# One planner change in a causal-attention-plus-gated-MLP kernel: the softmax sums' small constant added by a reduction, eight filler matmuls after the first scores, new TensorE costs and 66-column loads

## Chip, cores and metric

One NeuronCore of a Trainium2 chip runs the whole program. The metric is the device time of one execution in microseconds (us), lower is better; the time before is a median of three runs.

## What is computed

Causal attention over 4 batches, 12 heads, 448 positions and head size 64; the 12 heads' outputs, side by side, are the 768 inputs of a gated MLP with 1536 hidden units.

```python
scores = scale * np.matmul(q, k.transpose(0, 1, 3, 2))
scores = np.where(mask, -1000000000.0, scores)
scores = scores - np.max(scores, axis=-1, keepdims=True)
attn = np.exp(scores)
attn = attn / (np.sum(attn, axis=-1, keepdims=True) + 1e-09)
x = np.matmul(attn, v)            # heads side by side: (1792, 768)
g = x @ w_gate
out = (g * (1.0 / (1.0 + np.exp(-g))) * (x @ w_val)) @ w_out
```

All tensors are float32. The products are made either in plain f32 or from a high and a low part in the faster fp32r type ("split" products of three matmuls each).

## The kernel before

The work is cut into four chunks, one per batch (CHUNKS, line 23). A chunk first needs the attention of its 12 heads, and then the MLP on 448 columns. A "unit" is one head of one batch (48 units), and two neighbouring heads form a pair.

**Attention of a unit.** The 448 query rows are cut at 0, 64, 192, 320, 448. TensorE writes the scores of a pair into PSUM tiles S (lines 502 and 505; the two heads sit in different halves of the rows of the array, so their matmuls run side by side). In batch 0 the scores are plain f32 (tiles qraw and kraw); in batches 1 to 3 they are split products (QS and KS). The DVE adds the mask and takes the row maximum (lines 527 and 553, with a read-out of m), ACT takes the exponential and leaves each row's sum in one column of a shared tile (line 565, `sums`), and then `recip` (lines 573 to 577) makes the reciprocals. The normalisation p times rec runs on ACT, POOL or DVE (lines 592, 596, 609, 613). TensorE transposes p into PSUM tiles T (lines 667 and 699), these are copied out as ph (ACT or DVE, lines 311 and 314) with a low part pl (DVE, line 333), and the product with V goes to PSUM tile O (line 741, or 772 in batch 0).

`recip` is two DVE instructions on a 128x4 (or 128x3) piece:

```python
sm, rc = sums[u % NR][:, i0:i1], rec[u % NR][:, i0:i1]
nc.vector.tensor_scalar(rc, sm, 1.0e-9, None, ALU.add)
nc.vector.reciprocal(rc, rc)
```

**MLP of a chunk.** 24 blocks of gate and value weights and 12 of output weights, each of six k-steps; a k-step is three matmuls 128x448 (lines 874 to 876, PSUM tiles M and MO). In chunk 0 each weight block is loaded (wide, line 848), unpacked (top and wraw, lines 311 or 317 and 857), split into whl, and stored to DRAM; later chunks load the split form again (line 826).

**What sets the order.** A planner (class Planner, line 83) gets all operations with the engines on which each may run, a cost on each, a due time and dependencies, and places them greedily; the instructions are then issued in the planned order with no further reordering, each engine in its own fixed order. `cost` (line 62) prices an operation, TURN (line 42) adds a price on TensorE for going from one kind of work to another, CAPS gives the number of buffers. The T tiles of batches 1 to 3 share one PSUM bank: the next transposes wait until ph and pl of the last ones have been made.

**Start.** WARM = 22 small bf16 matmuls on a tile of ones (line 280) run on TensorE until the first q and k have been loaded; then come the scores of the first pair and those of the second. The first pair's scores are issued in three sessions (FIRST, line 53).

**Short loads.** Where only 64 columns of stationary operand are needed, FEW = 72 columns are loaded (lines 504 and 739): in the scores of the first query block of batches 1 to 3, and in the three products of each unit with pl.

Of the kernel before, what the change touches and what calls it, by code (L numbers as in the profile page):

```python
# [8 lines left out]
F32 = mybir.dt.float32  # L9
# [4 lines left out]
BF16 = mybir.dt.bfloat16  # L14
AF = mybir.ActivationFunctionType
ALU = mybir.AluOpType

P = 128
D = 64
# [1 line left out]
CUTS = [[0, 64, 192, 320, 448], [0, 64, 192, 320, 448], [0, 64, 192, 320, 448], [0, 64, 192, 320, 448]]  # L21
WID = [0, 64, 192, 320, 448]
CHUNKS = [[(0, 0, 448)], [(1, 0, 448)], [(2, 0, 448)], [(3, 0, 448)]]
NR = 8
SLOPE0 = 1.0
WLEAD = 1.2
XD = [-10.0, 3.0]
# [11 lines left out]
SHARED = 0.5  # L39
PVLATE = 0  # L40
LAT = {"PE": 0.29, "DVE": 0.2, "ACT": 0.23, "POOL": 0.2, "SP": 0.1}
TURN = {'ms': 0.19, 'sm': 0.19, 'mt': 0.0, 'tm': 0.0, 'ts': 0.19, 'st': 0.19, 'mv': 0.15, 'vm': 0.15, 'tv': 0.15, 'vt': 0.15, 'sv': 0.15, 'vs': 0.15, 'om': 0.055, 'os': 0.1, 'so': 0.19, 'ot': 0.03}
TS = 0.0
PF = 1.12
GF = 1.25
# [2 lines left out]
TV = 0.0  # L48
WINDOW = 96
SPARE = [2]  # L50
FEW = 72
WARM = 22
FIRST = [[[0, 1]], [[2]], [[3]]]
KBUS = 1 / 320
DLAT = 1.8
# [8 lines left out]
def cost(e, kind, n):  # L64
    if e == "ACT":
        return {"psum": 66, "sbuf": 110, "ptr": 190, "exp": 280, "tanh": 160}[kind] / 1e3 + n / 1200
    if e == "DVE":
        return 0.075 + n / {"one": 1920}.get(kind, 960)
    if e == "POOL":
        return {"one": 190, "ptr": 260, "two": 180}[kind] / 1e3 + n / {"two": 465.0}.get(kind, 1200.0)  # L70
    return {"r": max(n * 0.4475e-3 + 0.0025, 0.109), "n": n / 600, "t": n * 0.109 / 128}[kind] + 0.001


class Res:
# [154 lines left out]
def kernel(  # L229
# [8 lines left out]
    nc = tc.nc  # L238
# [3 lines left out]
    NW, _, WC = wP.shape  # L242
    NF = 12
    NKC = len(CUTS[0]) - 1
# [18 lines left out]
    masks = cpool.tile([P, P + maskX + P], F32, tag="masks", name="masks")  # L263
    back, mask = masks[:, : maskX + P], masks[:, P:]
    both = cpool.tile([P, D], F32, tag="both", name="both")
    all_sums = cpool.tile([P, NR, NKC], F32, tag="sums", name="sums")
    sums = [all_sums[:, i] for i in range(NR)]
    all_rec = cpool.tile([P, NR, NKC], F32, tag="rec", name="rec")
    rec = [all_rec[:, i] for i in range(NR)]
    xs = [cpool.tile([P, T], F32, tag=f"xs{i}", name=f"xs{i}") for i in range(KD)]  # L270
    xh = [cpool.tile([P, T], F32R, tag=f"xh{i}", name=f"xh{i}") for i in range(KD)]
# [4 lines left out]
    ones = xs[0][:, : P // 2]  # L276
    nc.vector.memset(ones, 1.0)
    warm = bank("O", "warm")
    for _ in range(WARM):
        nc.tensor.matmul(warm[:, :P], ones.bitcast(BF16), ones.bitcast(BF16), start=True, stop=True)  # L280
    cpool.tile([P, 32], F32, tag="pad", name="pad")
    top = cpool.tile([P, WC], U32, tag="top", name="top")
    nc.vector.memset(top, 0)
    nc.vector.memset(all_sums, 1.0)
    make_identity(nc, ident)
    nc.gpsimd.memset(masks, 0.0)
    for m_, step, base in ((back, 1, 1 - P), (mask, -1, maskX)):
# [10 lines left out]
    def op(alts, due, deps=(), alloc=(), uses=(), extra=0.0):  # L298
        first = [heads[r.tag] for r in alloc if r.tag in heads]
        o = pl_.op(alts, due, list(deps) + first, alloc, uses, extra)  # L300
        o.soft = first
        o.port = bool(alts.pop("port", False))
        o.kb = alts.pop("kb", 0)
        o.kind = alts.pop("kind", "m")
        for r in alloc:
            heads[r.tag] = o
        return o
# [84 lines left out]
    def attention(u):  # L392
# [76 lines left out]
        if h % 2 == 0:  # L469
            if not U.ns:  # L470
                rQ, rK = Res("QS"), Res("KS")
                sp = []
                for nm, r_, src, ld, rr in (("Q", rQ, "q", lq, rq), ("K", rK, "k", lk, rk)):
                    def newsp(nm=nm):
                        s[nm] = buf([P, 2, S], F32R, nm + "S", nm + "S", f"{nm}S{u}")
                        return s[nm][:, 0]
                    x1 = op(copies("sbuf", N, newsp, lambda src=src: s[src + "w"]), due(0), [ld], [r_], [rr])
                    sp.append(op(binary(N, lambda nm=nm: s[nm][:, 1], lambda src=src: s[src + "w"],
                                        lambda nm=nm: raw(s[nm])[:, 0]), due(1), [x1], [], [r_, rr]))
            for gi_, sess in enumerate(FIRST if rest else SG if c == 0 else [sum(SG, [])]):  # L480
                tags = ["S", "X"] if c else ["SXM"[gi_]] if rest else ["MS"[gi_ == 0]]
                rSs = {(y, x): Res(tags[x]) for x in range(len(sess)) for y in (0, 1)}
                steps = sorted(sum(sess, []))

                def score(gi_=gi_, sess=sess, steps=steps, tags=tags):
                    passes = ((None, None),) if U.ns else ((0, 0), (0, 1), (1, 0))
                    for x, blks in enumerate(sess):
                        for y in (0, 1):
                            B_, off = bank(tags[x], f"S{u + y}_{gi_}_{x}"), 0
                            for i in blks:  # L490
                                q1_ = U.qi[i][1][1]
                                st[u + y][f"S{i}"] = B_[:, off : off + q1_]
                                off += q1_
                    for i in steps:
                        q0, q1_ = U.qi[i][1]
                        for z, (a, b_) in enumerate(passes):
                            for y in (0, 1):
                                half = slice(D * y, D * y + D)
                                Q = s["qw"][half] if U.ns else s["Q"][half, a]
                                K = s["kw"][half] if U.ns else s["K"][half, b_]  # L500
                                if U.joint and i == 0:
                                    nc.tensor.matmul(st[u]["S0"][half], Q[:, :D], K[:, :D] if y else K[:, S - D :], start=True, stop=True)
                                    continue
                                r = max(U.rows[i], FEW)
                                nc.tensor.matmul(st[u + y][f"S{i}"][:r], Q[:, q0 : q0 + r],  # L505
                                                 K[:, :q1_] if y else K[:, S - q1_ :], start=z == 0, stop=z == len(passes) - 1)
                ws = [U.qi[i][1][1] for i in steps]
                if U.ns:
                    so = op({"PE": (sum(cost("PE", "n", w) + 0.06 for w in ws) + TS, score), "kind": "s"}, due(2),
                            (rest if gi_ else some) or [lq, lk], list(rSs.values()), [rq, rk])  # L510
                else:
                    so = op({"PE": (sum(3 * cost("PE", "r", w) for w in ws) + TS, score), "kind": "s"}, due(2), sp,
                            list(rSs.values()), [rQ, rK])
                for x, blks in enumerate(sess):
                    for i in blks:
                        for y in (0, 1):
                            scored[u + y, i] = (so, rSs[y, x])
# [54 lines left out]

        def recip():
            i0, i1 = U.own[0][0], U.own[-1][0] + 1
            sm, rc = sums[u % NR][:, i0:i1], rec[u % NR][:, i0:i1]
            nc.vector.tensor_scalar(rc, sm, 1.0e-9, None, ALU.add)
            nc.vector.reciprocal(rc, rc)  # L577
        rc = op({"DVE": (0.3, recip)}, due(5), exps, [], [rsum])

# [138 lines left out]
    def weigh(u):  # L718
# [6 lines left out]
        if not npv:  # L725
            rO, dps, use, dur = Res("O"), [], [], 0.0
            for g, o_, w, _, stk, d_, r_ in (blocks[j] for j in range(nj)):
                dps += [x for x in d_ if x not in dps]
                use += [r for r in r_ if r not in use]
                dur += (1 if stk else 2) * cost("PE", "r", w)  # L730

            todo = [(j, "ph") for j in (0, *range(2, nj))] + [(j, "pl") for j in range(nj - 1, 0, -1)] + [(1, "ph")]

            def pv():
                s["O"] = bank("O", f"O{u}")


                for x, (j, t) in enumerate(todo):
                    g, o_, w, _, stk, _, _ = blocks[j]
                    m = FEW if t == "pl" else 2 * D  # L740
                    nc.tensor.matmul(s["O"][:m, U.base(j) - U.qa : N], s["VS"][:, j, :m], s[f"{t}{g}"][:, o_ : o_ + w],  # L741
                                     start=x == 0, stop=x == len(todo) - 1)
            last = op({"PE": (dur, pv), "kind": "o"}, due(10), dps, [rO], use)
            rx, rt = Res(f"xs{h}"), Res("tmp")

            def newt():
                s["tmp"] = buf([D, S], F32, "tmp", "tmp", f"tmp{u}")[:, :N]
                return s["tmp"]
            t1 = op(copies("psum", N, newt, lambda: s["O"][D:P, :N], engines="AD"), due(11), [last], [rt], [rO])
            o = op(binary(N, lambda: xs[k][D * (h % 2) : D * (h % 2) + D, :N], lambda: s["O"][0:D, :N],  # L750
                          lambda: s["tmp"], ALU.add, engines="D"), due(12), [t1] + prevx, [rx], [rO, rt])
            xs_ops.setdefault((c, k), []).append(o)
            xs_res.setdefault((c, k), []).append(rx)
            return
# [261 lines left out]
```

## Time and profile before

| | us |
|---|---|
| median of 3 runs (lowest, highest) | 683.66 (683.42, 683.88) |
| the profiled execution | 684.65 |
| its span, first to last instruction | 682.9 |
| PE (TensorE matmul) busy | 671.8 |
| DVE busy | 356.7 |
| ACT busy | 347.8 |
| POOL (GpSimd) busy | 193.7 |

The profile is of one execution; its time is 0.99 us above the median and 1.75 us longer than its span. Matmuls are pipelined, so PE's busy share is not its distance from the peak: the spacing of the starts of two matmuls is what a matmul costs. A row of the timeline shows start, duration, engine, line, operation, tiles, shape, count, and in brackets how long the engine had been idle and who released it.

### The profile page before, as it was taken

How to read it: one execution, taken by the hardware profiler on the slowest of the kernel's cores; microseconds unless marked ns; L12 is line 12 of the kernel's file. 1: busy time of each engine (PE TensorE's matmuls, PEld its weight loads, DVE VectorE, ACT ScalarE, POOL GpSimd, SP SyncE). 2: the span in 40 equal slices, each digit the busy share in tenths (PEclk: the TensorE clock that was granted, in tenths of full speed). 3: DMA queues.
4: the chain of work that ended last, by engine and by line, in shares of the span. 5: the costliest groups of instructions: out<-in, count | busy, mean ns of one | idle time of the engine just before them, and what ended most of it. 6: DMA issues, size and time to landing. Idle time of an engine off the chain costs nothing.

```text
span 682.9 us, 10861 instructions
## 1 busy us (share of the span) xinstructions
PE 671.8 (98%) x3898; PEld 598.9 (88%) x3898; DVE 356.7 (52%) x881; ACT 347.8 (51%) x864; POOL 193.7 (28%) x238
## 2 busy tenths in 40 slices
PE   9999999999999999999999999999999999999998
PEld 6567898899888999999999989999999999999997
DVE  5777889898788464355633346545444222222100
ACT  6998688687798363245634336346345211111000
POOL 3766455556162130031322214134232000000000
PEclk9999999999999999999999999999999999999999
DMA  8878899999988865556667665554555675676771
GB/s 293 277 260 308 303 352 390 321 374 314 347 309 324 320 202 201 191 176 215 202 223 239 201 230 189 200 186 139 186 198 164 216 224 213 223 229 212 226 251 41
DMA packets 40118, 165.08 MB, mean 242 GB/s; under 512 B 4480, under 2 KB 13952, under 8 KB 40064
## 3 DMA queue, kind: packets, MB, share of 16 engines
q1 hardware_dynamic: 39904, 164.28, 70.6%
q8 instruction: 31, 0.51, 0.3%
q14 instruction: 23, 0.19, 0.1%
q10 hardware_dynamic: 160, 0.10, 0.1%
HBM read 130.55 MB, written 33.82 MB: 241 GB/s over the span
## 4 chain that ended last, share of the span: by engine, by line
PE 81%; ACT 11%; DVE 6%; issue 1%; POOL 0%; ACTq 0%; DVEq 0%
PE M L874 15%; PE M L875 15%; PE M L876 15%; PE MO L874 8%; PE MO L875 8%; PE MO L876 7%; PE S L505 4%; PE O L741 4%; ACT p L565 4%; PE T L699 3%; ACT p L609 2%; ACT ph L311 1%; ACT top L311 1%; DVE wraw L857 1%; PE T L667 1%
## 5 line engine op out<-in xcount | busy, mean ns | idle before, releaser
L874 PE MATMUL M<-xh,whl 128*128 128x448 f32 x576 | 215.0, 373 | 0.0
L875 PE MATMUL M<-xl,whl 128*128 128x448 f32 x576 | 209.4, 364 | 0.0
L876 PE MATMUL M<-xh,whl 128*128 128x448 f32 x576 | 209.1, 363 | 0.0
L874 PEld LDWEIGHTS M<-xh,whl 128*128 128x128 f32 x576 | 108.2, 188 | 8.5 <-issue 1.7
L876 PEld LDWEIGHTS M<-xh,whl 128*128 128x128 f32 x576 | 108.1, 188 | 7.7
L875 PEld LDWEIGHTS M<-xl,whl 128*128 128x128 f32 x576 | 108.4, 188 | 6.8 <-DVE xl L333 0.3
L874 PE MATMUL MO<-hh,whl 128*128 128x448 f32 x288 | 107.2, 372 | 0.0
L876 PE MATMUL MO<-hh,whl 128*128 128x448 f32 x288 | 104.6, 363 | 0.6 <-DVE whl L333 0.6
L875 PE MATMUL MO<-hl,whl 128*128 128x448 f32 x288 | 104.7, 364 | 0.0
L565 ACT ACTIVATE p<-p,m 128x192 f32<-128x192 f32 (+3 forms) x180 | 91.1, 509 | 3.4 <-DVE m L553 3.3
L311 ACT ACTIVATE ph<-T 128x384 fp32r<-128x384 f32 (+3 forms) x116 | 57.8, 504 | 56.5 <-PE T L667 34.4
L553 DVE CUSTOM_DVE_ANT_0 p<-S,masks 128x192 f32<-128x192 f32 (+3 forms) x180 | 68.3, 426 | 21.4 <-PE S L505 20.2
L311 ACT ACTIVATE hh<-t 128x448 fp32r<-128x448 f32 x40 | 23.1, 577 | 82.0 <-DVE t L917 82.0
L609 ACT ACTIVATE p<-p,rec 128x192 f32<-128x192 f32 (+3 forms) x130 | 58.8, 502 | 9.3 <-DVE rec L577 9.0
L911 DVE SCALAR_TENSOR_TENSOR t<-t,M 128x448 f32<-128x448 f32 x48 | 29.7, 619 | 57.2 <-ACT t L907 56.8
L876 PEld LDWEIGHTS MO<-hh,whl 128*128 128x128 f32 x288 | 54.0, 188 | 4.7 <-DVE whl L333 1.0
L874 PEld LDWEIGHTS MO<-hh,whl 128*128 128x128 f32 x288 | 54.1, 188 | 4.5 <-issue 1.2
L875 PEld LDWEIGHTS MO<-hl,whl 128*128 128x128 f32 x288 | 54.2, 188 | 3.6 <-DVE hl L333 0.3
L917 DVE TENSOR_TENSOR t<-t,M 128x448 f32<-128x448 f32 x48 | 29.6, 618 | 51.0 <-PE M L876 50.6
L907 ACT ACTIVATE t<-M 128x448 f32<-128x448 f32 x48 | 26.0, 542 | 57.5 <-PE M L876 56.9
L333 DVE TENSOR_TENSOR pl<-T,ph 128x384 fp32r<-128x384 f32 x72 | 39.6, 550 | 22.6 <-ACT ph L311 22.3
L699 PE MATMUL T<-ident,p 128*128 128x128 f32 x288 | 46.8, 276 | 3.3 <-DVE pl L333 3.0
(80 smaller groups left out, 822.7 us busy)
## 6 DMA issues: line engine op xcount, KB each, us to landing
whl<-ws SPq DMA_DIRECT2D x108, 768.0 KB, 4.4
wide<-in_w_dram SPq DMA_DIRECT2D x36, 768.0 KB, 6.8
ws<-whl SPq DMA_DIRECT2D x36, 768.0 KB, 7.5
vraw<-in_v_dram SPq DMA_DIRECT2D x24, 256.0 KB, 4.3
out_dram<-osb SPq DMA_DIRECT2D x24, 224.0 KB, 4.7
qraw<-in_q_dram SPq DMA_DIRECT2D x23, 224.0 KB, 4.6
kraw<-in_k_dram SPq DMA_DIRECT2D x23, 224.0 KB, 4.6
qraw<-in_q_dram SPq DMA_DIRECT2D x1, 128.0 KB, 2.5
```

The source lines that it names most:

```text
L311: nc.scalar.activation(out(), in_(), AF.Copy, scale=scale)
L333: r["DVE"] = (cost("DVE", "two", n), lambda: nc.vector.tensor_tensor(out(), a(), b(), alu))
L505: nc.tensor.matmul(st[u + y][f"S{i}"][:r], Q[:, q0 : q0 + r], K[:, :q1_] if y else K[:, S - q1_ :], start=z == 0, stop=z == len(passes) - 1)
L553: nc.vector.tensor_tensor_reduce(p[:r], s[f"S{i}"][:r], mask[:r, maskX - q0 : maskX - q0 + q1_] if h % 2 else back[:r, P - min(q1_, P) : P ...
L565: nc.scalar.activation(p[:r], p[:r], AF.Exp, bias=peak(i)[:r], scale=-1.0, accum_out=sums[u % NR][:r, i : i + 1],)
L609: nc.scalar.activation(p[:r], p[:r], AF.Copy, scale=rec[u % NR][:r, i : i + 1])
L699: nc.tensor.transpose(pt[:, o_ + q0 - bs : o_ + q0 - bs + r], s[f"p{i}"][:r, k0 : k0 + P], ident[:r, :r])
L874: nc.tensor.matmul(out[:, :n], a[:, w], xhi, start=first, stop=False)
L875: nc.tensor.matmul(out[:, :n], a[:, w], xlo, start=False, stop=False)
L876: nc.tensor.matmul(out[:, :n], l[:, w], xhi, start=False, stop=last)
L911: nc.vector.scalar_tensor_tensor(t, t, 1.0, ps[c, f, 0][:, :N], ALU.add, ALU.mult)
L917: nc.vector.tensor_tensor(t, t, ps[c, f, 1][:, :N], ALU.mult)
```

## The change

`recip` no longer adds 1e-9 with a tensor_scalar. The tile of sums gets one more slot that holds 1e-9 in every element, the ring of slots for units goes from 8 to 7 so that the tile keeps its size, and a tensor_reduce adds slot u % 7 and the last slot. Eight more of the small matmuls on ones are issued behind the scores of the first pair. FEW goes from 72 to 66. And the planner gets other numbers for TensorE: the TURN table, a price of 0.062 for score matmuls of 64 columns, and a price without a floor ("f") for the products with V.

```diff
-NR = 8
+NR = 7
-TURN = {'ms': 0.19, 'sm': 0.19, 'mt': 0.0, 'tm': 0.0, 'ts': 0.19, 'st': 0.19, 'mv': 0.15, 'vm': 0.15, 'tv': 0.15, 'vt': 0.15, 'sv': 0.15, 'vs': 0.15, 'om': 0.055, 'os': 0.1, 'so': 0.19, 'ot': 0.03}
+TURN = {'ms': 0.15, 'sm': 0.17, 'mt': 0.0, 'tm': 0.0, 'ts': 0.15, 'st': 0.17, 'mv': 0.15, 'vm': 0.15, 'tv': 0.15, 'vt': 0.15, 'sv': 0.15, 'vs': 0.15, 'om': 0.0, 'os': 0.1, 'so': 0.16, 'ot': 0.0}
-FEW = 72
+FEW = 66
 WARM = 22
+WARM2 = 8
-    return {"r": max(n * 0.4475e-3 + 0.0025, 0.109), "n": n / 600, "t": n * 0.109 / 128}[kind] + 0.001
+    return {"r": max(n * 0.4475e-3 + 0.0025, 0.109), "f": n * 0.4475e-3 + 0.0045, "n": n / 600, "t": n * 0.109 / 128}[kind] + 0.001
...
-    all_sums = cpool.tile([P, NR, NKC], F32, tag="sums", name="sums")
+    all_sums = cpool.tile([P, NR + 1, NKC], F32, tag="sums", name="sums")
...
-    for _ in range(WARM):
-        nc.tensor.matmul(warm[:, :P], ones.bitcast(BF16), ones.bitcast(BF16), start=True, stop=True)
+
+    def busy(n):
+        for _ in range(n):
+            nc.tensor.matmul(warm[:, :P], ones.bitcast(BF16), ones.bitcast(BF16), start=True, stop=True)
+
+    busy(WARM)
...
-    nc.vector.memset(all_sums, 1.0)
+    nc.vector.memset(all_sums[:, :NR], 1.0)
+    nc.vector.memset(all_sums[:, NR], 1.0e-9)
...
+                    if u == 0 and i in FIRST[-1][0]:
+
+                        busy(WARM2)
...
-                    so = op({"PE": (sum(3 * cost("PE", "r", w) for w in ws) + TS, score), "kind": "s"}, due(2), sp,
+                    so = op({"PE": (sum(3 * (0.062 if w == D else cost("PE", "r", w)) for w in ws) + TS, score), "kind": "s"}, due(2), sp,
...
-            sm, rc = sums[u % NR][:, i0:i1], rec[u % NR][:, i0:i1]
-            nc.vector.tensor_scalar(rc, sm, 1.0e-9, None, ALU.add)
+
+            sm, rc = all_sums[:, u % NR :: NR - u % NR, i0:i1], rec[u % NR][:, i0:i1]
+            nc.vector.tensor_reduce(rc, sm.rearrange("p a c -> p c a"), mybir.AxisListType.X, ALU.add)
             nc.vector.reciprocal(rc, rc)
...
-                dur += (1 if stk else 2) * cost("PE", "r", w)
+                dur += (1 if stk else 2) * cost("PE", "f", w)
```

The planner's new numbers move instructions on every engine. Three places follow, as the built programs have them; line numbers of the changed kernel are 3 to 10 higher than the same line before.

First, TensorE at the start, from the last scores of the first pair (S_2) to the first of the second pair (S_0). Before:

```order
L505 MATMUL S_1_0_262<-kraw_230,qraw_228 128x320
L505 MATMUL S_2_0_272<-kraw_230,qraw_228 128x448
L505 MATMUL S_2_0_273<-kraw_230,qraw_228 128x448
L502 MATMUL S_0_0_291<-kraw_240,qraw_238 64x64 x2
L505 MATMUL S_0_0_291<-kraw_240,qraw_238 128x448
```

and in the change, of which the first of eight load-and-matmul pairs on ones is shown:

```order
L511 MATMUL S_1_0_263<-kraw_231,qraw_229 128x320
L511 MATMUL S_2_0_273<-kraw_231,qraw_229 128x448
L511 MATMUL S_2_0_274<-kraw_231,qraw_229 128x448
L283 LDWEIGHTS xs_71
L283 MATMUL warm<-xs_71 128x128
```

Eight such pairs now stand between the two pairs' scores; the second pair's scores follow them in the same order as before.

Second, the DVE at units 36 and 37 (batch 3): the copy ph36_1 of the first transposes, then the reciprocals of unit 37, then the low part pl36_1, for which the next transposes T36_2 wait. Before:

```order
L314 TENSOR_SCALAR ph36_1_4682<-T36_1_4673 128x384
L576 TENSOR_SCALAR rec_70<-sums_69 128x4
L577 RECIPROCAL rec_70<-rec_70 128x4
L333 TENSOR_TENSOR pl36_1_4690<-T36_1_4673,ph36_1_4682 128x384
L314 TENSOR_SCALAR ph36_2_4706<-T36_2_4697 128x384
```

and in the change:

```order
L320 TENSOR_SCALAR ph36_1_4691<-T36_1_4682 128x384
L586 TENSOR_REDUCE rec_70<-sums_69 128x4
L587 RECIPROCAL rec_70<-rec_70 128x4
L339 TENSOR_TENSOR pl36_1_4699<-T36_1_4682,ph36_1_4691 128x384
L320 TENSOR_SCALAR ph36_2_4715<-T36_2_4706 128x384
```

The places in the row are the same; only the kind of the first instruction of `recip` differs.

Third, the DVE at unit 12 (batch 1, the first unit with split products). Before:

```order
L314 TENSOR_SCALAR ph12_1_1051<-T12_1_1043 128x384
L576 TENSOR_SCALAR rec_70<-sums_69 128x4
L577 RECIPROCAL rec_70<-rec_70 128x4
L333 TENSOR_TENSOR pl12_1_1059<-T12_1_1043,ph12_1_1051 128x384
L333 TENSOR_TENSOR whl5_992<-wraw5_903,whl5_992 128x768
L917 TENSOR_TENSOR t0_1_1028<-t0_1_1028,M0_3_1023 128x448
L333 TENSOR_TENSOR pl12_2_1090<-T12_2_1066,ph12_2_1082 128x384
```

and in the change, where ph12_1 is made on ACT:

```order
L339 TENSOR_TENSOR pl12_1_1082<-T12_1_1054,ph12_1_1062 128x384
L867 SCALAR_TENSOR_TENSOR wraw7_1088<-wide7_911,top_138 128x768
L339 TENSOR_TENSOR whl6_1075<-wraw6_1052,whl6_1075 128x768
L339 TENSOR_TENSOR pl12_2_1109<-T12_2_1090,ph12_2_1097 128x384
L586 TENSOR_REDUCE rec_70<-sums_69 128x4
L587 RECIPROCAL rec_70<-rec_70 128x4
```

The reciprocals have moved behind both pl; two instructions on weights (wraw7 and whl6) now stand between pl12_1 and pl12_2. On TensorE, 24 matmuls of the MLP stand between the transposes T12_2 and the next ones in the change.

## Rows read from the trace of the kernel before

**Rows 1.** Page: busy us (share) xcount; a stretch: its us, PE PEld DVE ACT POOL busy, clock.
```profile
PE 671.8 (98%) x3898; PEld 598.9 (88%) x3898; DVE 356.7 (52%) x881; ACT 347.8 (51%) x864; POOL 193.7 (28%) x238
...
12.60:46.00 33.40, 32.36 (x238) 19.73 (x240) 27.07 (x101) 32.67 (x103) 21.81 (x27) 1.00 0.85 297
```

**Rows 2.** Waits of PE: released by whom, total us, times, longest.
```profile
PE T L699 <- DVE pl L333: 3.0, 4, 1.4
PE O L741 <- DVE ph L333: 1.2, 2, 1.0
...
PE MO L876 <- DVE whl L333: 0.6, 1, 0.6
```

**Rows 3.** Timeline of PE at three of those four waits, last matmul before and transposes.
```profile
67.25 0.36 PE L875 MATMUL M<-xl,whl 128*128 128x448 f32 x1
67.45 0.36 PE L876 MATMUL M<-xh,whl 128*128 128x448 f32 x1
69.20 0.52 PE L699 MATMUL T<-ident,p 128*128 128x128 f32 x3 [1.40 <-DVE pl L333]
...
396.06 0.36 PE L876 MATMUL M<-xh,whl 128*128 128x448 f32 x1
...
397.06 0.52 PE L699 MATMUL T<-ident,p 128*128 128x128 f32 x3 [0.64 <-DVE pl L333]
...
502.17 0.36 PE L876 MATMUL MO<-hh,whl 128*128 128x448 f32 x1
502.81 0.30 PE L699 MATMUL T<-ident,p 128*128 128x128 f32 x1 [0.28 <-DVE pl L333]
```

**Rows 4.** Timeline of DVE and POOL at the same places.
```profile
66.78 1.62 DVE L576 TENSOR_SCALAR rec<-sums 128x4 f32<-128x4 f32 x1 [0.18 <-ACT p L565]
...
68.53 0.53 DVE L333 TENSOR_TENSOR pl<-T,ph 128x384 fp32r<-128x384 f32 x1
...
66.55 1.82 POOL L336 TENSOR_TENSOR whl<-wraw,whl 128x768 fp32r<-128x768 f32 x1
...
395.12 1.14 DVE L576 TENSOR_SCALAR rec<-sums 128x4 f32<-128x4 f32 x1
...
501.24 0.77 DVE L576 TENSOR_SCALAR rec<-sums 128x4 f32<-128x4 f32 x1
```

**Rows 5.** Lines 576 and 577: duration ns min/median/max, first and last start.
```profile
L576 DVE TENSOR_SCALAR rec<-sums x48: 151/170/1625, 9.3 to 527.8; 128x4 f32<-128x4 f32 x42, 128x3 f32<-128x3 f32 x6
...
L577 DVE RECIPROCAL rec<-rec x48: 175/178/179, 9.5 to 528.0; 128x4 f32<-128x4 f32 x42, 128x3 f32<-128x3 f32 x6
```

**Rows 6.** Timeline: a reciprocal on DVE while POOL runs.
```profile
31.64 0.18 DVE L577 RECIPROCAL rec<-rec 128x3 f32<-128x3 f32 x1
...
31.56 1.13 POOL L336 TENSOR_TENSOR xl<-xs,xh 128x448 fp32r<-128x448 f32 x1
```

**Rows 7.** Timeline of the start, and of later scores of the same shapes.
```profile
0.98 2.53 PE L280 MATMUL warm<-xs 128*128 128x128 bf16 x22 [0.98 <-DVE xs L277]
...
8.54 0.48 PE L502 MATMUL S<-kraw,qraw 64*64 64x64 f32 x4 [0.61 <-DVE m L553]
8.95 3.57 PE L505 MATMUL S<-kraw,qraw 64*128 64x448 f32 x12
...
12.55 0.36 DVE L553 CUSTOM_DVE_ANT_0 p<-S,masks 128x192 f32<-128x192 f32 x1 [0.64 <-PE S L505]
...
20.57 1.02 PE L505 MATMUL S<-kraw,qraw 64*128 64x448 f32 x4
...
22.76 1.13 PE L505 MATMUL S<-kraw,qraw 64*128 64x192 f32 x8
```

**Rows 8.** Loads for tile O by shape: duration ns min/median/max.
```profile
L741 PEld LDWEIGHTS O<-ph,VS x144: 186/188/190, 77.1 to 546.9; 128*128 128x128 f32 x144
...
L741 PEld LDWEIGHTS O<-pl,VS x108: 141/144/145, 77.6 to 546.8; 128*72 128x72 f32 x108
```

**Rows 9.** Timeline of DVE: a weight operation while POOL works on weights.
```profile
103.87 1.72 DVE L857 SCALAR_TENSOR_TENSOR wraw<-wide,top 128x768 uint32<-128x768 uint32 x1 [0.23 <-ACT top L311]
```

More of the change, by code (lines that the diff above doesn't have):

```diff
@@ L265 @@
     both = cpool.tile([P, D], F32, tag="both", name="both")
-    all_sums = cpool.tile([P, NR, NKC], F32, tag="sums", name="sums")
+    all_sums = cpool.tile([P, NR + 1, NKC], F32, tag="sums", name="sums")
     sums = [all_sums[:, i] for i in range(NR)]
-    all_rec = cpool.tile([P, NR, NKC], F32, tag="rec", name="rec")
+    all_rec = cpool.tile([P, NR + 1, NKC], F32, tag="rec", name="rec")
     rec = [all_rec[:, i] for i in range(NR)]
```

## The prediction

> **What bounds the kernel now.** I read the page first. TensorE (PE) is busy for 98% of the span, no other engine for more than 52% [rows 1], so the end is set by how closely matmuls follow each other and by what holds PE up. In the MLP two 128x448 matmuls start 0.20 us apart (67.25 and 67.45) [rows 3]; that work is the same before and after. What can change is the time in which PE stands still and the start. The early attention of batch 0 is the one stretch where another engine is as full as PE: ACT is busy 32.67 of 33.40 us [rows 1].
>
> Then the waits of PE. The longest entry is the transposes T waiting four times for pl, 3.0 us in all [rows 2]. The timeline shows three of the four: the matmul in front starts at 67.45, 396.06 and 502.17, the transposes 1.75, 1.00 and 0.64 us later, where 0.20 is normal [rows 3]. So PE loses 1.55, 0.80 and 0.44 us, 2.79 in all (more than the idle times in the brackets, which count from a modelled end).
>
> Why is pl late? The DVE's timeline answers: in front of pl stands the addition of 1e-9, a 128x4 instruction whose median is 0.17 us [rows 5] and which here takes 1.62, 1.14 and 0.77 us [rows 4]. At 66.78 it ends at 68.40, as POOL's subtraction does that began before it (66.55 + 1.82 = 68.37) [rows 4]. So the addition waits until POOL's instruction is over, and pl, which has nothing to do with it, waits in the DVE's queue behind it. The reciprocal, also small and from SBUF to SBUF, never takes more than 179 ns in 48 [rows 5], also while POOL is in the middle of an instruction [rows 6].
>
> The Trainium skill states a rule that fits ("SBUF — State Buffer", section on SBUF's two separate sides): DVE and GpSimd share one pair of ports as an exclusive lock, and a DVE instruction that uses both its ports waits until the other has finished. The trace agrees at 66.78, to within 0.03 us.
>
> **The change, part by part.** (a) **Reduction for addition.** No row of before shows a TENSOR_REDUCE. If it is held as the addition is, it saves nothing. If it runs free, like the reciprocal (0.18), the three holds shrink by 1.44, 0.96 and 0.59 us. PE then gets back no more than it lost: 1.44 + 0.80 + 0.44 = 2.68 us. At units 36 and 37 the queue of the DVE is otherwise the same; at unit 12 the reciprocals have moved away from pl altogether. Elsewhere the 48 additions lose (385 - 170) ns or so each by their mean, but PE does not stand still behind them, since MLP matmuls cover it; I give that nothing, with up to 0.4 as the far end. I take -2.7 (range 0 to -3.1), because the reciprocal is the nearest instruction: tiny, one input, SBUF to SBUF. The second memset and the slot ring of 7 cost nothing: the DVE waits for the first scores then, and a slot is needed again only seven units later.
>
> The skill also has a line against this edit ("VectorE: DVE Perf Modes", rules for kernel authors): a tensor_reduce is the slowest DVE operation and is better kept off a hot path. On 8 elements a row I would estimate from that page's half rate some 10 ns each, 0.5 us of DVE time over the 48, none of it on PE's path. The sum by that rule alone would be the same.
>
> (b) **Eight matmuls on ones.** The clock column reads 1.00 from the start, but the durations do not: the second pair's twelve score matmuls from 8.95 us take 3.57 us, and the same shapes later 1.02 + 1.13 = 2.15 us [rows 7]. So PE runs at its lower level (1.2 GHz) in the beginning, and it had stood still for 0.61 us before 8.54 [rows 7]. The 22 earlier fillers need 2.53 us, at most 0.115 each; eight take at most 0.92 us and fill that hole, and the second pair starts up to 0.3 us later. If the clock then rises during the second pair's scores, up to 3.57 - 2.15 = 1.42 us go. But after them ACT is full, and what the DVE stood waiting for PE is 0.64 us at 12.55 [rows 7]; that much shifts the whole chain, the rest (more than the 0.3 of delay) only turns into waiting for ACT. I take -0.6 (range +0.3 to -1.4).
>
> (c) **66 columns instead of 72.** A load of 128 columns lasts 188 ns, one of 72 columns 144 [rows 8]: 44 / 56 = 0.79 ns a column, 4.7 ns for six. In the scores 18 pairs times 3 passes (the two heads side by side) are 54 steps; there the matmul has only 64 columns, less than the load, so all of it shows: 0.25 us. In the products with V there are 108 such loads; behind matmuls of 256 and 384 columns they are mostly hidden, behind those of 128 not: 36 x 4.7 = 0.17 us. Sum -0.4 (range 0 to 162 x 4.7 = -0.8).
>
> (d) **Planner's prices.** They move instructions on all engines but add none. On TensorE the number of turns between kinds of work hardly changes, so the pure work is equal. The remaining stalls (O behind ph 1.2, MO behind whl 0.6 [rows 2], one of the T waits) come from instructions on the DVE standing in a bad place behind POOL, and a new order throws these dice again: 0, plus or minus 1.5.
>
> (e) **Given back.** PE will be some 2 us earlier by 200 us (0.6 of b, 1.44 of a). There it already waits 0.6 us once for split weights [rows 2], so part of the lead may be lost while weights are still being unpacked: +0.5 (range 0 to 2).
>
> Sum: -2.7 - 0.6 - 0.4 + 0 + 0.5 = -3.2 us against the profiled 684.65, which gives 681.4 for an execution with a profile; that one lies 0.99 us above the median, so 683.66 - 3.2 = **680.5**. A measurement of this kernel can tell about 0.2% (1.4 us) from no change; this is 0.47%.
>
> **The rivals.** *The clock does not rise sooner.* Then b costs some 0.2 instead of saving 0.6: 681.3, still faster. For it: PE had run its fillers and the first pair's scores for almost 7 us without the clock rising, so one filled hole may not be what was missing. Against it: the hole is the longest stop in that stretch. The Trainium skill ("TensorE: Matmul & The Clock Gate", part 1) speaks for it: the check behind the clock runs on its own time, not from the kernel's start, so that the same kernel sees a different number of slow matmuls from run to run. One trace of before can't bear that out.
>
> *The change doesn't do what it says: the reduction is held too.* Then only b and c stay: 683.66 - 0.6 - 0.4 = 682.7, within 0.2%. Against it stand the 48 reciprocals [rows 5, 6].
>
> *The gain is given back* by late weights (e at its far end) or by one or two new stalls: -3.7 + 2 + 1 = -0.7, 683.0, also within 0.2%. For it: DVE and ACT are full in the first stages.
>
> *Slower.* The new order can put an instruction with two SBUF inputs, which POOL holds up, in front of what PE needs. One such, wraw at 103.87 [rows 9], took 1.72 us and cost PE about 1.0 (the longest wait of O for ph [rows 2]). In the change wraw7 and whl6 stand between pl12_1 and pl12_2. There it is covered: 24 MLP matmuls, 4.8 us, stand before the next transposes, against two such holds of 1.7 and a pl of 0.5. It decides from five uncovered ones on: 5 x 1.0 - 3.7 = +1.3, and with e +1.8, 685.5. Against it: before, with DVE as full, only four stops of PE for DVE were of another kind than a's (two of O, one of MO, one of T) [rows 2].
>
> **How the numbers follow.** Forecast with the clock's share 0.50 (680.5, own range 677.5 to 682.2), without it 0.24 (681.3), reduction held 0.06, given back 0.12, slower 0.08. The first two are faster by over 0.2%, with a little of the next two: 0.76. Same 0.16, slower 0.08. The range goes from 677.5 (a, b, c near their far ends and a lucky order) to 683.2, which takes in most of the cases given back; slower and the tails are left out, together about 0.18.
>
> **What would show it.** Right: line 586 at most 0.25 us in all 48 while POOL runs beside it; T behind pl near 0.7 instead of 3.0 us in the waits of PE; the second pair's twelve scores well under 3.57 us and the DVE's 0.64 us wait gone; short loads near 139 ns. Wrong: a TENSOR_REDUCE that ends when POOL does; new waits of PE for ph, pl or whl of over 2 us together; a wait for whl around 200 us that grows by what was gained before it.

## The result and the profile after

| | before | after |
|---|---|---|
| median, us (lowest, highest; runs) | 683.88 (683.42, 685.04; 5) | 690.13 (688.83, 690.27; 5) |
| profiled execution | 684.65 | 690.13 |
| its span | 682.9 | 688.4 |
| first transposes T of batch 0 start at | 12.45 | 11.51 |

The change makes the kernel slower: the ratio is 1.0085 (95% interval 1.007 to 1.010), 6.2 us, where 3.2 us less were forecast. The last row splits the profiled spans of 682.9 and 688.4 us: up to the first T the change gains 0.9 us, and from there to the end it loses 676.9 - 670.5 = 6.4 us. Of all the executions recorded here two took 1.7 ms, one of the kernel before and one with the reduction alone, and they have no part in any ratio below.

The page after, busy time by engine (answers to [rows 1]):

```profile
PE 675.5 (98%) x3906; PEld 597.9 (87%) x3906; DVE 357.3 (52%) x902; ACT 338.7 (49%) x844; POOL 186.7 (27%) x238
```

PE has 3.7 us more of busy time for eight small fillers of some 0.1 us each. Something that PE always did now takes longer. The waits of PE after (released by whom, total us, times, longest) answer to [rows 2]:

```profile
PE MO L886 <- DVE whl L339: 1.6, 2, 1.3
PE T L677 <- DVE pl L339: 1.3, 1, 1.3
PE T L709 <- DVE pl L339: 1.0, 3, 0.6
...
PE S L511 <- DVE m L562: 0.9, 1, 0.9
PE T L677 <- POOL p L623: 0.7, 1, 0.7
PE O L782 <- ACT ph L317: 0.7, 1, 0.7
PE T L709 <- DVE m L562: 0.7, 1, 0.7
```

At line 699, now 709, the waits of T for pl fell from 3.0 to 1.0 us. But the transposes of line 677 now wait 1.3 us for pl, and five other waits stand beside these. So the waits that the reduction was to remove became smaller, and its gain is gone again. That the reduction runs free shows in its own line after, and in the DVE and POOL rows around 308 us, where it runs in the middle of a subtraction of POOL's:

```profile
L586 DVE TENSOR_REDUCE rec<-sums x48: 143/156/165, 10.0 to 529.3; 128x4 f32<-128x8 f32 x42, 128x3 f32<-128x6 f32 x6
```

```profile
308.04 0.15 DVE L586 TENSOR_REDUCE rec<-sums 128x4 f32<-128x8 f32 x1
```

```profile
308.03 1.16 POOL L342 TENSOR_TENSOR hl<-t,hh 128x448 fp32r<-128x448 f32 x1
```

All 48 take 143 to 165 ns, where the addition took up to 1625 [rows 5].

A loss nearly as large as the whole difference is in the MLP's stream of matmuls. Here is the timeline of PE after at 548.8, behind the last product with V:

```profile
548.47 0.52 PE L751 MATMUL O<-pl,VS 128*66 128x128 f32 x3
548.83 0.34 PE L751 MATMUL O<-ph,VS 128*128 128x384 f32 x1
549.00 0.37 PE L884 MATMUL MO<-hh,whl 128*128 128x448 f32 x1
549.21 0.37 PE L885 MATMUL MO<-hl,whl 128*128 128x448 f32 x1
549.42 0.37 PE L886 MATMUL MO<-hh,whl 128*128 128x448 f32 x1
...
684.58 0.36 PE L886 MATMUL MO<-hh,whl 128*128 128x448 f32 x1
```

and the same place before:

```profile
547.12 0.33 PE L741 MATMUL O<-ph,VS 128*128 128x384 f32 x1
547.29 0.36 PE L874 MATMUL MO<-hh,whl 128*128 128x448 f32 x1
547.49 0.36 PE L875 MATMUL MO<-hl,whl 128*128 128x448 f32 x1
547.69 0.36 PE L876 MATMUL MO<-hh,whl 128*128 128x448 f32 x1
...
679.09 0.36 PE L876 MATMUL MO<-hh,whl 128*128 128x448 f32 x1
```

Before, the last 660 matmuls start (679.09 - 547.29) / 659 = 0.2000 us apart; after, the last 657 start (684.58 - 549.00) / 656 = 0.2067 us apart. The stream has **two rhythms, 200 and 206.7 ns**, and in both of these stretches it keeps its rhythm to the end. The tail alone costs 656 x 6.7 ns = 4.4 us more. Over the whole kernel I added, for two MLP matmuls that follow each other 195 to 215 ns apart, what is above 200 ns: 1.8 us before (213 of 2371 distances of 205 ns or more), 7.7 us after (1115 of 2379). This excess grew by 5.9 us. The new slow stretches are those behind products with V: of the stretches with more than three matmuls, 15 of 20 have a mean distance over 204 ns after, 1 of 19 before, and their part of the excess went from 0.1 to 6.4 us. Behind transposes some short stretches (9 to 39 matmuls) are slow in both kernels, 18 of 84 before and 17 of 80 after.

The loads of that group did get shorter, 137 instead of 144 ns:

```profile
L751 PEld LDWEIGHTS O<-pl,VS x108: 134/137/140, 76.8 to 548.5; 128*66 128x66 f32 x108
```

### The profile page after: what moved, and what is told of

It reads as the page before. It is cut to its first block, busy times and chain, and to the rows that moved or that the text cites. A ratio compares the mean times of both kernels' runs of the same rounds, so it can differ in the third digit from the quotient of the medians.

```text
span 688.4 us, 10886 instructions
## 1 busy us (share of the span) xinstructions
PE 675.5 (98%) x3906; PEld 597.9 (87%) x3906; DVE 357.3 (52%) x902; ACT 338.7 (49%) x844; POOL 186.7 (27%) x238
## 4 chain that ended last, share of the span: by engine, by line
PE 79%; ACT 9%; DVE 7%; issue 2%; DMA 2%; POOL 0%; ACTq 0%; DVEq 0%
PE M L884 14%; PE M L885 14%; PE M L886 14%; PE MO L884 7%; PE MO L885 7%; PE MO L886 7%; PE S L511 4%; PE O L751 4%; PE T L709 3%; ACT p L574 3%; ACT p L619 2%; DVE wraw L867 2%; DVE whl L339 2%; PE O L782 1%; DMA wide<-in_w_dram 1%
## 5 line engine op out<-in xcount | busy, mean ns | idle before, releaser
L317 ACT ACTIVATE ph<-T 128x384 fp32r<-128x384 f32 (+3 forms) x96 | 48.2, 512 | 64.5 <-PE T L709 32.7
L317 ACT ACTIVATE hh<-t 128x448 fp32r<-128x448 f32 x44 | 25.3, 575 | 84.9 <-DVE t L927 84.9
L619 ACT ACTIVATE p<-p,rec 64x64 f32<-64x64 f32 (+3 forms) x122 | 54.9, 508 | 5.7 <-DVE rec L587 5.7
L623 POOL TENSOR_SCALAR p<-p,rec 128x448 f32<-128x448 f32 (+3 forms) x58 | 36.5, 637 | 63.5 <-DVE rec L587 47.9
```

Of the source, the lines that this page charges most:

```text
L317: nc.scalar.activation(out(), in_(), AF.Copy, scale=scale)
L619: nc.scalar.activation(p[:r], p[:r], AF.Copy, scale=rec[u % NR][:r, i : i + 1])
L623: nc.gpsimd.tensor_scalar(p[:r], p[:r], rec[u % NR][:r, i : i + 1], 0.0, ALU.mult, ALU.add)
```

## Experiments

FEW is no part of the planner's costs, so the number of columns can be changed without moving one instruction; the reduction and the fillers leave the order of all else as it was, too. That lets each part be tried alone. In round brackets stands the ratio to the kernel before, timed beside each run, with its 95% interval.

**Columns alone, in both directions.**

```diff
-FEW = 66
+FEW = 72
```

> The changed kernel with loads of 72 columns again, the same order of instructions otherwise. Theory R (rhythm): behind the products with V the matmul stream of the MLP falls into starts 206.7 ns apart instead of 200 because of the 66-column loads; with 72 the excess over 200 ns falls from 7.7 us to some 2 us, and the time to 684.2 (range 683.0 to 685.5). Rival O (order): the planner's new order makes the rhythm and the stalls, the short loads nothing; then 690 stays (with 162 loads 5 ns longer, 690.5).

> The kernel before with loads of 66 columns, the same order of instructions otherwise. Theory R: the runs of MLP matmuls behind the products with V start 206.7 ns apart, some 900 of them, 6 us more: 689.5 (range 687 to 691). Rival O: 683.5, since only the loads get 5 ns shorter (0.4 us).

Measured: the changed kernel with 72 columns 684.83 us (ratio to before 1.0009, 1.0000 to 1.0018), the kernel before with 66 columns 688.87 (1.0073, 1.0061 to 1.0085). Excess over 200 ns: 1.66 and 8.38 us. The end of the stream with 72 columns in the changed order, then with 66 in the old:

```profile
546.77 0.36 PE L884 MATMUL MO<-hh,whl 128*128 128x448 f32 x1
546.97 0.36 PE L885 MATMUL MO<-hl,whl 128*128 128x448 f32 x1
547.17 0.36 PE L886 MATMUL MO<-hh,whl 128*128 128x448 f32 x1
```

```profile
547.42 0.37 PE L874 MATMUL MO<-hh,whl 128*128 128x448 f32 x1
547.63 0.37 PE L875 MATMUL MO<-hl,whl 128*128 128x448 f32 x1
547.84 0.37 PE L876 MATMUL MO<-hh,whl 128*128 128x448 f32 x1
```

So the rhythm comes from the 66 columns, in either order: +5.3 and +5.0 us. The rival, the order, is out for this part. But 684.83 is also not below before: the reduction's gain must be lost elsewhere.

**The reduction alone** (old order, 72 columns):

```diff
-NR = 8
+NR = 7
...
-            nc.vector.tensor_scalar(rc, sm, 1.0e-9, None, ALU.add)
+            nc.vector.tensor_reduce(rc, sm.rearrange("p a c -> p c a"), mybir.AxisListType.X, ALU.add)
```

The lines left out are those of the change for the tile of sums.

> The kernel before with the reduction in place of the addition, alone; order, prices, fillers and loads as before. If part (a) of the prediction was right, the reduction is never held by POOL, the three waits of the transposes for pl at 67, 396 and 502 us shrink from 2.8 us of lost time to about 0.1, and the time is 681.2 (range 680.8 to 682.0). Rival: the time in front of the transposes is given back at once by the next wait (weights, O or T), then 683 or more.

> The kernel with the reduction alone once more, for its profile. Measured so far: 678.1 us, 5.8 below the kernel before, where the prediction had 2.7 for this part. Theory A: the three waits of the transposes (2.8 us) are gone, and the rest is the matmul stream's: with the transposes in time the slow rhythm behind T (excess 1.8 us before) falls as well, and later waits for ph, whl shrink by some 1 us. Theory B: the additions were held at many more places than the three in the waits' list, each under 0.4 us (48 additions lose some 10 us on the DVE), and these together are worth 3 us on PE; then the rhythm's excess stays at 1.8 us and the waits outside the three fall by 3 us.

Measured: 678.10 (0.9915, 0.9902 to 0.9928) and 677.97 us (0.9917, 0.9904 to 0.9931), 5.8 us below before, twice what I had forecast and below the range of my expectation. Its waits of PE, all of them:

```profile
PE warm L280 <- DVE xs L277: 1.0, 1, 1.0
PE S L503 <- DVE m L554: 0.9, 1, 0.9
PE O L742 <- DVE ph L334: 0.8, 1, 0.8
PE MO L877 <- DVE whl L334: 0.2, 1, 0.2
PE O L773 <- DVE ph L315: 0.2, 1, 0.2
```

Excess 2.2 us: the rhythm has no part in it. From the first T to the end it needs 665.4 us against 670.5 before: 5.0 to 5.1 less, and the rest of what the span lost lies in the start, which varies (below). TensorE has the same instructions in the same order in both traces, so each start can be compared with its counterpart. The three waits of [rows 3] give 1.56 + 0.80 + 0.44 = 2.8. Three more places give 1.6: 0.42 us at 204 us, 0.39 at 214 and 0.81 at 218; the rest is spread thin. At the first of them a held addition stood well ahead of the place where PE waited. DVE and then PE, before:

```profile
199.16 0.59 DVE L576 TENSOR_SCALAR rec<-sums 128x4 f32<-128x4 f32 x1
...
202.11 1.91 DVE L333 TENSOR_TENSOR whl<-wraw,whl 128x768 fp32r<-128x768 f32 x1
```

```profile
204.06 0.47 PE L876 MATMUL MO<-hh,whl 128*128 128x448 f32 x1 [0.62 <-DVE whl L333]
```

From 199.16 to 202.11 the DVE has no idle time, so the 0.42 us (0.59 - 0.17) by which the addition is late arrives at whl, and PE waits 0.62. With the reduction the same instruction of PE waits 0.19. At 214 it is an addition of 1.01 us, for whose reciprocals ACT's normalisation waits; the copy ph and then O on PE come behind that:

```profile
209.81 1.01 DVE L576 TENSOR_SCALAR rec<-sums 128x4 f32<-128x4 f32 x1 [0.19 <-ACT p L565]
211.12 1.15 ACT L609 ACTIVATE p<-p,rec 64x64 f32<-64x64 f32 x3 [0.61 <-DVE rec L577]
```

The place at 218 is another matter. There the fourth of the waits of T for pl is gone, because whl on the DVE, held by POOL before, is not held in this execution. First DVE and PE before, then the same whl with the reduction:

```profile
215.17 1.72 DVE L333 TENSOR_TENSOR whl<-wraw,whl 128x768 fp32r<-128x768 f32 x1
218.36 0.55 PE L699 MATMUL T<-ident,p 128*128 128x128 f32 x3 [0.65 <-DVE pl L333]
```

```profile
210.23 0.94 DVE L334 TENSOR_TENSOR whl<-wraw,whl 128x768 fp32r<-128x768 f32 x1
```

That is luck of timing: of the eight traces here with the reduction in the old order, six have this whl at 1.72 or 1.73 us again. So theory B holds in part: held additions elsewhere cost PE time, and the waits outside the three shrank, but not all of the surplus is theirs.

**Fillers beside the reduction** (old order, 72 columns):

```diff
+                    if u == 0 and i in FIRST[-1][0]:
+                        busy(WARM2)
```

> The kernel before with the reduction and the eight fillers behind the first pair's scores; order, prices and 72 columns as before. By the prediction's part (b) the fillers are worth 0.6 us: 677.5 (range 676.7 to 678.4). Rival: what the start gains is waited for later, since ACT is full in batch 0; 678.1 as with the reduction alone.

Measured: 678.59 (0.9923, 0.9909 to 0.9936). No gain over the reduction alone can be seen, 0.5 us too much if anything. (In the two traces this run is 0.7 us later at the first T, and it has the wait at 218 us again.) The start explains why nothing is gained. After, with fillers:

```profile
8.39 1.04 PE L283 MATMUL warm<-xs 128*128 128x128 bf16 x8
9.36 0.40 PE L508 MATMUL S<-kraw,qraw 64*64 64x64 f32 x4
9.69 1.89 PE L511 MATMUL S<-kraw,qraw 64*128 64x448 f32 x12
```

and with the reduction alone, without any:

```profile
8.69 1.89 PE L506 MATMUL S<-kraw,qraw 64*128 64x448 f32 x12
```

The twelve scores that took 3.57 us in the one execution shown of before [rows 7] take 1.89 in this one without a filler. Over the kernels profiled here, eight with fillers have 1.89 to 2.10 us in these scores; of eleven without, six have 3.57, four 1.89 and one 2.42. So with the fillers the twelve scores were short in every trace, without them in about half. These eleven are not eleven sure draws: all five from two of the chips used have 3.57, all five from three others 1.89 to 2.42 (the eleventh is before's profile, 3.57), so the chip or the hour may matter as well as the execution. The mean start of the first T goes only from 11.7 (10.5 to 12.7) to 10.9 us (10.3 to 11.5).

**Which short loads, and how short** (reduction and fillers, old order). The edit for the products with V:

```diff
-                    m = FEW if t == "pl" else 2 * D
+                    m = 66 if t == "pl" else 2 * D
```

and likewise with 64, 68 and 80, FEW being 72; for the scores alone FEW is 66 and m is 72.

> Reduction and fillers, and 66 columns only in the scores of the first query block (54 steps); the products with V load 72. Theory R (the loads in front of the MLP's matmuls set the rhythm): no slow stretches, 0.25 us less than with 72 everywhere: 677.3. Rival: any 66-column load shifts the phase: 681 or more.

> Reduction and fillers, and 66 columns only in the 108 loads of the products with V; the scores load 72. Theory R: the slow rhythm is back behind the products, 900 gaps or more at 206.7 ns, 5 to 6 us more than with 72 everywhere: 683 (range 682 to 684). Rival: 677.4.

> Reduction and fillers, with 64 columns in the loads of the products with V. If the rhythm depends on short loads below some width between 66 and 72, it is slow: 683 to 684.5, some 900 gaps at 206.7 ns behind the products. If 66 is a matter of phase alone, it may be either; at 200 ns it is 678.0.

> The same with 68 columns. Below the width that decides: 683 to 684.5; above it: 678.3. A time between would say that only a part of the runs of matmuls falls into the slow rhythm.

> Reduction and fillers, with 80 columns in the loads of the products with V (72 in the scores). If the slow rhythm is a matter of 66 against more columns, 80 keeps starts 200 ns apart behind the products: some 6 ns more for each of 108 loads, 679.0. If it comes and goes with the length of the loads (a phase), 80 may fall into it: 683 to 685 with 900 gaps at 206.7 ns.

| columns in scores, products with V | us | distances of 205 ns or more, excess |
|---|---|---|
| 72, 72 | 678.59 | 232, 1.96 us |
| 66, 72 | 678.24 | 224, 1.86 us |
| 72, 66 | 683.64 | 997, 7.08 us |
| 72, 64 (one run) | 679.09 | 272, 2.25 us |
| 72, 68 (one run) | 678.54 | 158, 1.53 us |
| 72, 80 (one run) | 678.43 | 223, 1.93 us |

All of the loss comes from the products with V, and of five widths only 66 has it: 64 and 68 on either side are free of it. My reading that there is a width below which the stream turns slow is wrong. That it is a matter of phase, of the moment at which the group of products ends, fits but is not shown. In the last stretch the first MLP matmul behind the products starts 174 ns behind the last of them with 66 columns, 175 with 64 and with 80, 181 with 68, 171 with 72; the distance to the second is 206 ns with 66, 204 or 205 with 64, 68 and 80, and 200 with 72, and it then settles at 206.7 ns with 66 and at 200 with the others. With 66 columns the slow rhythm is not certain either: in that trace, of 17 stretches of more than one matmul behind the products, eleven begin 174 or 175 ns behind the products and are slow, six begin 177 or 178 ns behind and settle at 200. With 64 columns they begin 173 to 175 ns behind and settle at 200, so that delay alone does not select. What does stays open.

**The order alone** (new prices, nothing else; then with the reduction):

> The kernel before with the planner's new prices alone, which gives the order of the changed kernel; 72 columns, no reduction, no fillers. Theory R: no slow stretches behind the products with V; but the addition is held by POOL again at other places, and the new order's waits for whl, pl and ph come on top: 685.5 (range 684.0 to 687.5). Rival O: the order alone makes the loss, 690 to 693.

> The reduction and all the new prices, 72 columns, no fillers: the new order without the fillers. If the order alone costs what it did with them (684.8 against 678.6): 684.3, 6.2 above the reduction alone. If the fillers have a part in it: 682 or less.

Measured: 689.44 (1.0078, 1.0065 to 1.0091) and 684.83 (1.0008, 0.9995 to 1.0020). The first lies above my range and just under the rival's; the second is as expected, and as long as with the fillers. The planner's new numbers cost 5.6 us without the reduction (689.44 - 683.88) and 6.8 with it (684.83 - 678.0; 6.2 by the ratios); with reduction and fillers it is 684.83 - 678.59 = 6.2. The excess of the rhythm is 1.83 and 1.71 us, so the order does not make the rhythm: this loss is waiting. The waits of PE in the changed kernel with 72 columns, without the two of the start:

```profile
PE MO L886 <- DVE whl L339: 1.4, 2, 1.1
...
PE T L677 <- DVE pl L339: 1.3, 1, 1.3
PE T L709 <- DVE pl L339: 1.1, 3, 0.6
...
PE S L511 <- DVE m L562: 0.9, 1, 0.9
PE T L677 <- POOL p L623: 0.7, 1, 0.7
PE O L782 <- ACT ph L317: 0.7, 1, 0.7
```

All waits of that list but the two of the start sum to 7.4 us, those of the same parts in the old order (reduction, fillers, 72 columns), again without the start, to 1.6. The two longest single waits are 1.32 and 1.13 us. The second, in that kernel's timelines of DVE and PE:

```profile
199.58 0.54 DVE L320 TENSOR_SCALAR ph<-T 128x384 fp32r<-128x384 f32 x1
200.05 1.43 DVE L867 SCALAR_TENSOR_TENSOR wraw<-wide,top 128x768 uint32<-128x768 uint32 x1
...
203.07 0.16 DVE L586 TENSOR_REDUCE rec<-sums 128x4 f32<-128x8 f32 x1 [0.84 <-ACT p L574]
...
203.36 0.99 DVE L339 TENSOR_TENSOR whl<-wraw,whl 128x768 fp32r<-128x768 f32 x1
```

```profile
204.41 0.47 PE L886 MATMUL MO<-hh,whl 128*128 128x448 f32 x1 [1.13 <-DVE whl L339]
```

The new order puts the reciprocals of a unit in front of whl, and they wait 0.84 us for ACT's exponentials; PE's output stream waits 1.13 us behind them. In the old order, with reduction and fillers too, PE waits 0.2 us in all for whl. The first has the same form: the subtraction for QS waits 1.23 us for ACT, pl stands behind it on the DVE, and T waits for pl:

```profile
226.45 0.63 DVE L339 TENSOR_TENSOR QS<-qraw,QS 128x448 fp32r<-128x448 f32 x1 [1.23 <-ACT QS L317]
226.99 0.55 DVE L339 TENSOR_TENSOR pl<-T,ph 128x384 fp32r<-128x384 f32 x1
```

```profile
227.60 0.66 PE L677 MATMUL T<-ident,p 128*128 128x128 f32 x4 [1.32 <-DVE pl L339]
```

**Which price, and is it any other order?** On the reduction alone:

> The kernel with the reduction (678.0 us), 72 columns, no fillers, and of the new prices the TURN table alone. The new order as a whole costs some 6 us on top of the reduction (684.8 against 678.6 with fillers). Theory P (these prices): cheaper turns between kinds of work let the planner believe that PE comes sooner, and it puts more on the DVE (907 instead of 884 instructions); TURN alone gives most of the loss: 682 to 685, and the other two prices alone under 1.5. Theory D (any other order): the order of before is one that fits, and each of the three edits that shuffles it costs 2 us or more: 680 to 685 here.

> The kernel with the reduction and of the new prices the one without a floor for the products with V alone (the smallest shuffle: 176 rows of TensorE differ, 892 instructions on the DVE). Theory P: under 1.5 us more than 678.0. Theory D: 680 to 684.

> The kernel with the reduction and of the new prices the 0.062 for score matmuls of 64 columns alone (886 instructions on the DVE). Theory P: under 1.5 us more than 678.0. Theory D: 680 to 684.

> The kernel with the reduction (678.0 us) and the TURN prices moved the other way, up by 0.02 to 0.055 us; nearly as many rows of TensorE differ as with the new prices. If any other order costs (theory D): 680 to 684. If it is the lower prices (theory P): 677.5 to 679.

> The kernel with the reduction and one price that is not TensorE's moved by a little (the planner's latency of a transfer, 1.8 to 1.85 us): 110 rows of TensorE differ. Theory D: 679.5 or more. Theory P: 677.5 to 679.

| edit to the planner | us | ratio to before (interval) |
|---|---|---|
| none | 677.97 | 0.9917 (0.9904 to 0.9931) |
| TURN as in the change | 680.76 | 0.9950 (0.9932 to 0.9968) |
| price without a floor ("f") | 679.15 | 0.9929 (0.9914 to 0.9945) |
| 0.062 for scores of 64 columns | 680.30 | 0.9947 (0.9932 to 0.9962) |
| TURN moved up | 679.02 | 0.9914 (0.9889 to 0.9939) |
| transfer latency 1.8 to 1.85 | 678.36 | 0.9911 (0.9895 to 0.9928) |

TURN moved up shuffles nearly as many rows as the change does and, by the ratios, costs nothing that these intervals show; neither does the latency. So not every other order is bad, and theory D falls as it stands. Of the three new prices two do cost, but not as theory P had it: 2.3 (TURN), 0.8 ("f", not clear of nothing) and 2.1 us (scores) by the ratios, so TURN is not most of it, and the price for scores is above the 1.5 us that P allowed. Their sum is 5.2 against 6.2 for all three by the same measure, which is no difference at these intervals. Whether lower prices cost as such, or some of these five orders are bad draws, five orders do not show. I followed only two waits, in the order of all three prices; what each price moves to make the others stays open.

**What beats both kernels.** The reduction with 66 columns in the scores alone, old prices, no fillers:

> The kernel before with the reduction and 66 columns in the scores alone; the products with V load 72, old prices, no fillers. By the runs so far the reduction is worth 5.8 us and the short score loads 0 to 0.3: 677.8 (range 677.2 to 678.4), 0.9% below the kernel before. Rival: no gain over the reduction alone, 678.1.

Measured: 677.93 (0.9913, 0.9900 to 0.9927), 6.0 us below before and 12.2 below after's median, and not to be told from the reduction alone.

## Why the prediction was wrong

The forecast failed at **two steps, (c) and (d)**: each gives back about what the reduction gained. Of its marks for the right side three stood (the 48 reductions, the short loads at 137 ns, the second pair's scores at 1.89 us); T behind pl did not fall to 0.7 us, but to 1.0 at the old line, with 1.3 at another. Of the marks for the wrong side two stood, new waits of PE of over 2 us and the longer wait for whl.

- (a) Reduction, forecast -2.7, measured -5.8. The mechanism was right: never held, and the three waits gone for 2.8 us. The size was off in part because I priced only those additions that stood directly in front of a wait of PE ("PE does not stand still behind them, since MLP matmuls cover it"): two held additions reached PE some 5 us later, along a full DVE and through ACT, for 0.4 us each. Of the rest of the profile's gain, 0.8 us was luck at 218 us, and the start varies. The Trainium skill's lock ("SBUF — State Buffer", SBUF's two separate sides) binds a DVE instruction that uses both its ports; that none of the 48 reductions took more than 165 ns fits an instruction outside it. The line of the Trainium skill against a tensor_reduce ("VectorE: DVE Perf Modes", rules for kernel authors) cost nothing here: 156 ns by the median against 170 for the addition.
- (b) Fillers, forecast -0.6, measured +0.5, not to be told from none. The 3.57 us were one draw; I took a single execution for the rule. That the same kernel sees a different number of slow matmuls from run to run was the rival's ground (the Trainium skill, "TensorE: Matmul & The Clock Gate", part 1). The eleven traces without fillers agree in that the same scores take 3.57, 2.42 or 1.89 us, though they do not separate the execution from the chip.
- (c) **Short loads, forecast -0.4 with 0 as the worst end, measured +5.0 to +5.3.** The loads shrank as worked out (144 to 137 ns), the scores' part is at most a few tenths. The failed step is "that work is the same before and after", said of the MLP's 0.20 us: with 66 columns in the products with V, the stream of hundreds of matmuls behind them runs at 206.7 ns. The term had no positive end because I held the 200 ns for a constant of the work.
- (d) **Prices, forecast 0 plus or minus 1.5, measured +5.6 to +6.8.** I held a new order for a throw of dice around zero. Its three edits alone came out at +0.8 to +2.3 and all three at about +6, so the center was wrong, not only the spread. The rival "slower" had the right place (DVE instructions in front of what PE needs) and too small a price, 1.8 us. Its mechanism, two-input instructions held by POOL, is not what makes the two waits that were followed: there DVE instructions that wait for ACT stand in front of whl and of pl. Its count of "only four stops" was short, too: in the same list of before O of line 772 waits 0.6 us for ph and S 0.6 for m, both made on the DVE.
- (e) Weights near 200 us, forecast +0.5. The wait did grow, from 0.6 to 1.3 us (1.6 with a second one); it belongs to (d), since with the reduction in the old order it shrank to 0.2.

As a chain of measured medians: 683.88, with the reduction 678.10 (-5.8), with the fillers 678.59 (+0.5), with the new order 684.83 (+6.2), with 66 columns 690.13 (+5.3). Before's own median was 683.8 to 683.9 beside each of them.

## What to carry to other kernels

When the spacing of a long stream of equal instructions is the bound, read it in several stretches before taking it for a constant: if two values occur, ask what stands in front of each, since a change of a few ns there can move hundreds of instructions. Change the cost table of a greedy planner apart from every other edit, and compare the waits that its new order makes, even if its prices look better. And a held instruction can be paid for not only where the next one waits, but some us later: here two additions reached PE 5 us behind, one along a DVE without idle time, one through ACT.

## What the hardware showed that I had not expected

- Matmuls of 128x448 with a 128-column load each run at 200 or at 206.7 ns from start to start, and a stretch can stay in either for as long as it is unbroken (660 matmuls in the longest case); behind the products with V the first few distances already differ. Of load widths 64, 66, 68, 72 and 80 in those products, only 66 leads into the slow one. Behind transposes short slow stretches occur with 72 columns, too.
- The same twelve score matmuls at the start take 3.57 us in one trace and 1.89 in another, near the factor between TensorE's two levels, 1.2 and 2.4 GHz, while the column of the granted clock says 1.00 in both. That the clock rises at another point is read from these durations alone.
